# A sequence layer with an FFT convolution and a dense layer: the second norm's epsilon moves from VectorE to GpSimd, and all instructions stand in another order

## The chip, the core and the metric

The kernel runs on one core of one Trainium2 chip. The metric is the time of one execution in microseconds (us) of device time; less is better. The core's engines are named as the profile names them: PE is TensorE (matmuls; PEld its weight loads), DVE is VectorE, ACT is ScalarE, POOL is GpSimd, SP is SyncE, which here issues nearly all DMAs.

## What is computed

There are 2048 rows of 640 channels, all bf16. The reference, cut to its core:

```python
def _layernorm(x, eps=1e-5):
    return (x - mean(x)) / sqrt(var(x) + eps)

def _A_ref(q, k, v, shift_k, ssm_k, ssm_D):
    k_shift = sum(k_pad[:, t:t + S, :] * shift_k[:, ks - 1 - t] for t in range(4))
    kv = k_shift * v
    y = causal_convolution(kv, ssm_k)          # written as rfft, product, irfft over 2 * S
    return q * (y + kv * ssm_D)

def _B_ref(x, w1, b1, w2):
    h = x @ w1 + b1                            # 640 -> 1728
    return (h * tanh(softplus(h))) @ w2        # mish, 1728 -> 640

x = A_q
h = x + _A_ref(_layernorm(x), A_k, A_v, A_shift_k, A_ssm_k, A_ssm_D)
return h + _B_ref(_layernorm(h), B_w1, B_b1, B_w2)
```

So there is a first norm (of x), a long convolution, a gate and a sum, a second norm (of h), and a dense layer with Mish.

## The kernel before

The convolution is a Fourier transform in matmuls. The channels are cut into five chunks of 128. The stages, with the names that the order uses for their operations (`pe` at the end is the TensorE part, `ev` the copy of its PSUM result to SBUF, the eviction):

- **k1**: the filter `ssm_k` is transposed, one operation a chunk (L374).
- **s1k**: the first transform of the filter, 20 operations of 16 matmuls (L394, L395), each with an eviction of 128x1024.
- **kt**: the rows of `k` are transposed, 5 chunks of 8 fp32 transposes (L339), each chunk with one eviction of 2048 bf16 columns (`ktev`). **ks** makes the shifted sum, 10 operations of 16 matmuls (L355, L356); **kv** multiplies it with `v` on VectorE (L360), 10 operations. `wsh` and `ktsh` on GpSimd prepare both.
- **s2k**: a multiplication of all chunks of the filter with a table G, 22 operations of 6 matmuls (L420; the last has 2), evictions of 128x960 (the last 128x320). It needs all 20 s1k evictions.
- **s1v**, **s2v** (named s2v0, s2v1, s2v2 after the chunks they hold): the same two steps for the products k v, 20 operations each, evictions of 128x1024.
- **sw**: ten DMAs swap halves of the filter's spectrum; they need all s2k evictions. **pr**: 20 spectral products on VectorE (L459).
- **i1** (L477, 20 operations with evictions of 128x1024) and **i2** (L529, one for each of 16 tiles of 128 rows, eviction `y` of 128x640): the way back. i2 needs all i1.
- Per tile t: **ln1_t** takes the first norm's statistics on VectorE (L508, L509), **ln1p** turns them into a scale and a bias on GpSimd (L513 adds epsilon, L514 raises to the power -0.5, L515), **lnx** applies them (ScalarE L520 or GpSimd L522). **wb** and **h** (L536, L538) gate and add. **bn** takes the second norm's statistics (L542, L543) and adds epsilon (L544, VectorE), **pow** raises to -0.5 (L546, GpSimd), **hc** normalizes (L548, VectorE). Tiles 0 and 1 are transposed on TensorE (`trpe`, evicted by `trev`), the others by DMA (`tr`, L561).
- Dense layer: units of 256, 256, 512, 512, 512 rows. **m1** (L586, L593) is the first matmul, seven operations a unit, **hb** (L608) Mish on ScalarE, **m2** (L651, L659) the second matmul, **res** (L673, L676) the last sum on VectorE, **d_out** the store.

The order is one list, `ORDER`. Each word is an operation; all instructions are issued in the order of the list, each on its engine, and every engine works through its own in that order. `@n` gives the PSUM buffer of a TensorE operation: there are four, each 1024 fp32 columns wide, and a buffer is free for the next `@n` when the eviction of the one before has ended. `:d`, `:a`, `:p` put an operation on VectorE, ScalarE or GpSimd; without a letter an eviction of s1, s2, i1 or i2 runs on ScalarE. So the list decides which engine evicts what, which buffer is waited for, and in which order the DMAs are issued (SP too works through its own in order).

```python
EV = ["act", "dve"]
o.eng = _LETTER[eng] if eng else o.engs[0]
if o.psum is not None:
    o.psum.slot = int(slot)
```

Of the kernel before, what the change touches and what calls it, by code (L numbers as in the profile page):

```python
# [34 lines left out]
s2kev_18 kv1_0 kspe4_0@3 s2kev_12 s2kpe_90@1 kv4_0 s2kpe_54@0 s2kev_90 kspe3_1@2 s2kev_54 s2kpe_60@3 kv3_1 s1vpe0_3@1 s2kev_60 s2kpe_78@0 kspe2_1@2
s1vev0_3 s2kev_78:d s2kpe_102@3 s2kpe_0@1 kv2_1 s2kev_102 kspe2_0@0 s2kev_0 s2kpe_66@3 d_x3 kv2_0 s1vpe1_3@2 s2kev_66 s1vpe3_2@1 s1vev1_3:d d_x1
s1vpe3_0@0 s1vev3_2 s1vpe1_1@3 d_x0 d_x2 s1vev3_0 s1vev1_1:d s1vpe0_0@2 s2kpe_120@1 s1vev0_0 s1vpe2_2@0 s2kev_120:d s1vpe1_2@3 s1vev2_2 s1vpe2_0@2
s1vev1_2:d s1vpe1_0@1 s1vev2_0 s2kpe_6@0 d_t2m s2kpe_72@3 s1vev1_0 s2kev_6:d s2kpe_48@2 s2kev_72 s2kpe_96@1 s2kev_48:d s2v0pe_16@0 s2kev_96 s2kpe_84@3
s2v0ev_16:d s2kpe_30@2 s2kev_84 s1vpe4_2@1 ln1_3 s2kev_30 s2kpe_42@0 s2kpe_126@3 s2kev_42 s2kev_126:d s2kpe_108@2 ln1p3 ln1_0 s1vpe4_1@3 s2kev_108
s1vpe4_0@0 s1vev4_1:d s1vev4_2 ln1p0 s1vpe4_3@2 sw0_0 sw0_1 s1vev4_0 s1vev4_3:d s1vpe2_3@1 sw3_0 s1vpe3_3@3 lnx3:p s1vev2_3 sw1_1 s1vpe3_1@0  # L40
s1vev3_3:d s1vpe2_1@2 sw4_1 s1vev3_1 s2v0pe_0@1 lnx0:p sw2_1 ln1_1 s2v0pe_96@3 s1vev2_1 sw1_0 s2v0pe_80@0 sw3_1 ln1_2 s2v0ev_96 ln1p1 s2v0pe_64@2
sw2_0 s2v0ev_80 s2v0ev_0:d sw4_0 s2v0pe_32@3 lnx1:p s2v0ev_64 s2v0pe_112@0 pr0_0 ln1p2 s2v0pe_48@1 s2v0ev_112 s2v2pe_0@2 s2v0ev_32:d lnx2:p s2v0ev_48
s2v2pe_112@0 pr0_64 s2v2ev_112 s2v2pe_80@3 s2v1pe_64@1 s2v2ev_0 pr0_96 s2v2ev_80 s2v2pe_96@0 pr0_32 s2v2pe_32@2 s2v2ev_96 s2v2pe_64@3 pr1_96 s2v2ev_64
s2v2pe_16@0 pr1_64 s2v2ev_32 i1pe0_0@3 s2v1ev_64 s2v2pe_48@2 pr1_32 s2v2ev_48 i1pe0_3@1 pr1_0 s2v2ev_16 s2v1pe_0@2 pr3_32 i1ev0_0 s2v1pe_96@0 i1ev0_3
pr3_96 s2v1pe_32@3 s2v1ev_0 pr3_64 i1pe0_2@1 d_w12 s2v1ev_32 d_w11 i1pe0_1@2 pr4_96 d_w10 i1ev0_2 d_w13 i1pe1_2@3 pr3_0 d_w14 i1ev0_1 i1pe1_3@1
i1ev1_2 pr2_64 i1pe1_0@2 s2v1ev_96 pr2_0 i1pe3_0@3 i1ev1_3 i1pe3_2@0 pr2_32 i1ev1_0 i1pe3_1@1 pr4_64 i1ev3_0 i1pe3_3@2 i1ev3_1 pr2_96 i1pe1_1@3
# [4 lines left out]
hc2 pow3 y9 m1pe0_1@0 ln1_12 tr2 y5 w2z hb0_0 m1pe0_4@1 hc3 wb9 ln1p5 tr3 hb0_1 wb4 m1pe0_2@2 hb0_4 ln1_11 ln1p8 lnx5 m1pe0_5@3 wb7 hb0_2 ln1p12
ln1_10 m1pe0_6@0 hb0_5 m1pe1_6@1 h4 ln1p11 lnx12 ln1_15 m1pe1_0@2 hb1_6 ln1p10 ln1_14 lnx11 m1pe1_3@3 bn4 hb0_6 ln1p15 hb1_0 m1pe1_5@1 hb1_3 wb5
m1pe1_2@0 h7 hb1_5 wb6 h6 m1pe1_4@2 lnx15:p hb1_2 bn7 pow4 m1pe1_1@3 hb1_4 h5 pow7 hc4 i2pe11@1 bn6 hb1_1 ln1p14 tr4 i2pe12@0 m2pe0@2 y12 h9 lnx14:p
hc7 lnx10 bn9 pow6 y11 lnx8 hc6 pow9 bn5 tr6 m2pe2@3 wb14 pow5 tr7 hc9 wb10 wb11 tr9 wb8 hc5 h10 tr5 h8 wb15 bn8 m2pe1@0 h11 pow8 bn10 hc8 pow10 res0
m1pe2_6@1 h15 d_out0 ln1_13 tr8 m1pe2_1@2 hc10 ln1p13 hb2_6 res2 tr10 bn11 lnx13:p m1pe2_3@3 h14 hb2_1 pow11 wb12 hc11 h12 tr11 bn15 m2pe3@1 hb2_3
d_out2 wb13 pow15 bn14 hc15 pow14 bn12 tr15 m1pe3_6@2 h13 pow12 bn13 m1pe2_0@3 hc14 pow13 hb3_6 res3 res1 d_out3 hc12 d_out1 m1pe2_4@1 hc13 tr14 hb2_0
tr13 m1pe3_4@2 hb2_4 tr12 m1pe2_2@0 hb3_4 m1pe3_1@3 hb2_2 m1pe3_5@1 hb3_1 m1pe2_5@2 m1pe3_3@0 hb2_5 m1pe3_0@3 hb3_3 hb3_5 m1pe3_2@2 hb3_0 m2pe5@0
hb3_2 m2pe7@1 m2pe4@3 res7 res5 d_out7 d_out5 m2pe6@2 m1pe4_0@1 res6 res4 d_out4 d_out6 m1pe4_2@0 hb4_0 m1pe4_6@2 m1pe4_1@3 hb4_6 hb4_2 m1pe4_3@1
# [110 lines left out]
def kernel(  # L169
# [333 lines left out]
    for t in range(NT):  # L503
# [36 lines left out]
        def bnf(e, t=t):  # L540
            for hh in range(2):
                nc.vector.bn_stats(st2[:, t, hh, :], xt(t)[:, hh * 320:(hh + 1) * 320])  # L542
            nc.vector.bn_aggr(mv2[:, t, :], st2[:, t, :, :])  # L543
            nc.vector.tensor_scalar(ve2[:, t:t + 1], mv2[:, t, 1:2], EPS, None, ALU.add)  # L544
# [1 line left out]
        o_pw = OP(f"pow{t}", "pool", [o_bn, o_small], emit=lambda e, t=t: nc.gpsimd.tensor_tensor(r2[:, t:t + 1], ve2[:, t:t + 1], mhalf[:], ALU.pow))  # L546
        o_hc = OP(f"hc{t}", "dve", [o_pw] + ([trs[t - 7]] if t >= 7 else list(ks_pes.values())),
                  emit=lambda e, t=t: nc.vector.tensor_scalar(hc_s[t % 7], xt(t), mv2[:, t, 0:1], r2[:, t:t + 1], ALU.subtract, ALU.mult))  # L548
# [173 lines left out]
```

## Time and profile before

| what | us |
|---|---|
| median of 3 runs (lowest, highest) | 226.48 (226.25, 226.64) |
| the profiled execution's own time | 226.59 |
| its span, first to last instruction | 224.7 |
| first matmul of m1 starts | 99.94 |
| first matmul of m2 starts | 116.73 |
| last res starts | 221.78 |

A table by stage gives, for a stretch of time, the busy time of each engine, the number of its instructions behind an x, the granted TensorE clock, the busy share of the DMA engines and what they moved. A timeline row gives start, duration, engine, line, operation, output and inputs with shapes, and how many such instructions are merged in it; in brackets stands how long the engine idled ahead of it and what ended the wait. A group row has, behind the bar, the busy time of the group, the mean in ns of one, and idle time ahead of it. A matmul's printed duration holds its way through the array, so matmuls overlap: the distance from start to start is what one costs. The granted clock is 1.00 in all stretches.

### The profile page before, as it was taken

How to read it: one execution, taken by the hardware profiler on the slowest of the kernel's cores; microseconds unless marked ns; L12 is line 12 of the kernel's file. 1: busy time of each engine (PE TensorE's matmuls, PEld its weight loads, DVE VectorE, ACT ScalarE, POOL GpSimd, SP SyncE). 2: the span in 40 equal slices, each digit the busy share in tenths (PEclk: the TensorE clock that was granted, in tenths of full speed). 3: DMA queues.
4: the chain of work that ended last, by engine and by line, in shares of the span. 5: the costliest groups of instructions: out<-in, count | busy, mean ns of one | idle time of the engine just before them, and what ended most of it. 6: DMA issues, size and time to landing. Idle time of an engine off the chain costs nothing.

```text
span 224.7 us, 6128 instructions
## 1 busy us (share of the span) xinstructions
PE 214.4 (95%) x2644; PEld 157.3 (70%) x2650; DVE 137.6 (61%) x250; ACT 131.6 (59%) x178; POOL 58.5 (26%) x106
## 2 busy tenths in 40 slices
...
GB/s 177 386 414 416 417 369 16 139 340 276 417 417 18 274 125 158 254 0 58 5 29 76 59 98 67 128 18 0 3 0 58 40 21 0 0 20 29 88 29 73
DMA packets 19563, 30.98 MB, mean 138 GB/s; under 512 B 10704, under 2 KB 14928, under 8 KB 18768
## 3 DMA queue, kind: packets, MB, share of 16 engines
...
q10 hardware_dynamic: 336, 0.12, 0.3%
...
## 4 chain that ended last, share of the span: by engine, by line
PE 65%; DVE 11%; ACT 10%; DMA 6%; POOL 3%; issue 2%; SPq 0%; DVEq 0%; POOLq 0%
PE ps L651 26%; PE ps L586 22%; ACT uv L259 8%; DVE ks L459 6%; DMA rb<-in_A_q_dram 4%; PE ps L394 3%; DMA ks<-in_A_ssm_k_dram 2%; PE ps L339 2%; PE ps L355 2%; PE ps L420 2%; PE ps L374 2%; PE ps L356 2%; PE ps L395 1%; PE ps L593 1%; PE ps L659 1%
## 5 line engine op out<-in xcount | busy, mean ns | idle before, releaser
L608 ACT ACTIVATE ks<-ps,b1s 128x512 bf16<-128x512 f32 (+1 forms) x69 | 36.2, 599 | 47.9 <-PE ps L586 30.7
L651 PE MATMUL ps<-ks 128*128 128x320 bf16 (+2 forms) x420 | 58.6, 299 | 0.0
L586 PE MATMUL ps<-G 128*128 128x512 bf16 (+1 forms) x319 | 57.5, 336 | 0.8 <-ACT ks L608 0.5
L651 PEld LDWEIGHTS <-ks 128*128 128x128 bf16 x420 | 40.6, 98 | 17.4 <-issue 1.3
L586 PEld LDWEIGHTS <-G 128*128 128x128 bf16 x325 | 31.2, 98 | 25.3 <-issue 1.3
L259 ACT CAST uv<-ps 128x1024 bf16<-128x1024 f32 x49 | 45.7, 1099 | 0.1
L676 DVE TENSOR_TENSOR rb<-ps,rb 128x640 bf16<-128x640 f32 x15 | 11.8, 820 | 50.5 <-PE ps L659 48.1
L259 ACT CAST ks<-ps 128x960 bf16<-128x960 f32 (+2 forms) x46 | 37.7, 912 | 7.9 <-PE ps L395 5.9
L459 DVE TENSOR_TENSOR ks<-ks,uv 128x2048 bf16<-128x2048 bf16 x20 | 23.4, 1239 | 0.0
L420 PEld LDWEIGHTS <-G 128*128 128x128 bf16 x512 | 20.6, 96 | 3.6 <-issue 2.9
L477 PE MATMUL ps<-a_t,ks 128*128 128x128 bf16 x320 | 19.0, 219 | 0.9 <-ACT uv L259 0.5
L477 PEld LDWEIGHTS <-ks 128*128 128x128 bf16 x320 | 18.4, 113 | 1.5 <-issue 0.5
L513 POOL TENSOR_SCALAR ve<-mv 128x1 f32<-128x1 f32 x16 | 4.6, 289 | 47.7 <-DVE mv L509 46.7
L546 POOL TENSOR_TENSOR r<-ve,mhalf 128x1 f32<-128x1 f32 x16 | 10.8, 675 | 16.9 <-DVE ve L544 16.8
L420 PE MATMUL ps<-uv,G 128*128 128x64 bf16 (+1 forms) x384 | 12.7, 186 | 1.7 <-ACT uv L259 1.3
L508 DVE BATCH_NORM_STATS2 st<-rb 128x6 f32<-128x320 bf16 x32 | 13.8, 472 | 0.8 <-DMA rb<-in_A_q_dram 0.8
L542 DVE BATCH_NORM_STATS2 st<-rb 128x6 f32<-128x320 bf16 x32 | 14.0, 480 | 0.1
L261 DVE CAST ks<-ps 128x1024 bf16<-128x1024 f32 (+2 forms) x12 | 13.2, 1127 | 1.4 <-PE ps L395 0.7
L261 DVE CAST uv<-ps 128x1024 bf16<-128x1024 f32 x11 | 13.1, 1205 | 0.1
L673 DVE TENSOR_TENSOR rb<-ps,rb 128x384 bf16<-128x384 f32 (+1 forms) x2 | 1.0, 492 | 19.9 <-PE ps L651 19.9
L360 DVE TENSOR_TENSOR ra<-ps,rb 128x1024 bf16<-128x1024 f32 x10 | 11.9, 1219 | 1.3 <-PE ps L356 0.7
L522 POOL TENSOR_SCALAR ra<-rb,r,nmr 128x640 bf16<-128x640 bf16 x10 | 12.1, 1212 | 1.2 <-PE ps L395 0.6
...
## 6 DMA issues: line engine op xcount, KB each, us to landing
...
G<-in_B_w_dram SPq DMA_DIRECT2D x5, 432.0 KB, 5.5
```

What stands on the lines that cost most here:

```text
L259: nc.scalar.copy(o, i)
L261: nc.vector.tensor_copy(o, i)
L360: nc.vector.tensor_tensor(kv_w[:, m, :, 8 * h:8 * h + 8, :], p_.f32().rearrange("p (l t d) -> p d t l", l=4, t=8), raw_v[:, 8 * h:8 * h + ...
L420: nc.tensor.matmul(p_.f32()[:, o:o + n], g_v[:, f, :], src[:, :, f, :], start=True, stop=True)
L459: nc.vector.tensor_tensor(o, o, v, ALU.mult)
L477: nc.tensor.matmul(pz[:, dgl, :], KS[:, k, b, :, l], a12[:, k, :], start=k == 0, stop=k == 1)
L508: nc.vector.bn_stats(st1[:, t, hh, :], xt(t)[:, hh * 320:(hh + 1) * 320])
L522: nc.gpsimd.tensor_scalar(lnx_s[t % 9], xt(t), r1[:, t:t + 1], nmr1[:, t:t + 1], ALU.mult, ALU.add)
L542: nc.vector.bn_stats(st2[:, t, hh, :], xt(t)[:, hh * 320:(hh + 1) * 320])
L586: nc.tensor.matmul(ph[:, o:o + w], w1[:, dc, fc * P:fc * P + P], lt[:, dc, 0:w], start=dc == 0, stop=dc == NDC - 1)
L608: nc.scalar.activation(hb[:, fc, 0:n], p_.f32()[:, i * 512:i * 512 + n], ACT.Mish, bias=b1s[:, fc:fc + 1], scale=1.0)
L651: nc.tensor.matmul(p_.f32()[:, o:o + n], lhs, w2[:, k, cols:cols + n], start=fc == 0, stop=single and fc == 13)
```

## The change

The addition of epsilon in `bn` goes from VectorE (L544) to GpSimd, in front of the power, where the first norm has it already. `hc` gets a second form on ScalarE, which the constant `HC_ACT = ()` leaves unused.

```diff
-            nc.vector.tensor_scalar(ve2[:, t:t + 1], mv2[:, t, 1:2], EPS, None, ALU.add)
         o_bn = OP(f"bn{t}", "dve", [o_h], emit=bnf)
-        o_pw = OP(f"pow{t}", "pool", [o_bn, o_small], emit=lambda e, t=t: nc.gpsimd.tensor_tensor(r2[:, t:t + 1], ve2[:, t:t + 1], mhalf[:], ALU.pow))
...
+        def pwf(e, t=t):
+            nc.gpsimd.tensor_scalar(ve2[:, t:t + 1], mv2[:, t, 1:2], EPS, None, ALU.add)
+            nc.gpsimd.tensor_tensor(r2[:, t:t + 1], ve2[:, t:t + 1], mhalf[:], ALU.pow)
+            if t in HC_ACT:
...
+        o_pw = OP(f"pow{t}", "pool", [o_bn, o_small], emit=pwf)
```

The whole list `ORDER` is another one: the same 660 operations in other places, with other buffers and, in part, other engines. Its first part, up to the first operations of s1v, reads before and after:

```diff
-d_dr wz idn d_n0 cz wm@0 small lane d_n1 d_cst d_sk d_n2 warm d_n4 d_n3 kz d_g7 dsel dcol dadd0 d_k0 k1pe0@1 dadd1:p d_k3 k1pe1@2 d_k1 k1ev0b d_k2
-k1ev0 s1kpe0_2@3 k1ev1 s1kpe0_1@0 s1kev0_2 dadd2:p d_v2 s1kpe0_0@1 s1kev0_1 s1kpe1_2@2 dadd4:p d_a12 s1kpe0_3@3 s1kev1_2:d k1pe2@0 s1kev0_3 d_v1 dadd3
...
-s1kpe4_0@2 s1kev2_2 s1kpe2_0@3 s1kev4_0:d d_g2 s1kpe3_2@0 s1kev2_0 s1kpe3_3@1 wsh2 s1kev3_2:d s1kpe3_0@2 d_g1 ktpe4_0@3 s1kev3_0 ktpe4_3 s1kev3_3:d
-ktpe4_1 ktpe1_0@0 ktpe1_1 ktpe1_3 d_g3 ktpe1_2 ktpe4_2 ktev1:a ktpe0_0@2 ktev4 ktpe0_2 ktpe0_1 ktpe2_0@1 d_g0 ktpe0_3 ktpe2_2 ktev0 s1kpe4_3@3 d_g5
...
-kv0_0 s1kpe2_3@2 s1kpe4_2@1 kv0_1 s1kev2_3 ktsh3 kspe4_1@3 ktsh2 s1kev4_2 s1kpe3_1@2 kv4_1 s1vpe0_2@0 s1kev3_1 s1kpe2_1@1 s1vev0_2:d s1vpe0_1@3
-s1kev2_1 kspe1_1@2 s1vev0_1 s2kpe_36@0 kv1_1 s2kpe_114@1 s2kev_36 kspe3_0@3 s2kev_114:d s2kpe_24@2 kspe1_0@0 s2kev_24 kv3_0 s2kpe_18@1 s2kpe_12@2
+d_dr wz idn d_n0 cz wm@0 small lane d_n1 d_cst d_sk d_n2 warm d_n3 d_n4 d_g0 dsel dcol dadd0 d_k2 k1pe0@1 d_k3 dadd1:p k1pe1@2 d_a12 k1ev0b d_k0 k1ev0
+s1kpe0_3@3 k1ev1 s1kpe0_1@0 s1kev0_3 d_k1 s1kpe0_0@1 dadd2 s1kev0_1 s1kpe1_3@2 s1kev0_0:d dadd3:p d_g4 s1kpe0_2@3 k1pe2@0 s1kev0_2 dadd4:p d_g1
+s1kev1_3 kz b1pe@1 k1pe4@3 k1ev2 c_b1 cfpe@2 k1pe3@1 k1ev4:a coef d_v0 s1kpe2_0@0 k1ev3 wsh1 s1kpe2_1@2 s1kev2_0 s1kpe4_3@3 d_g7 s1kev2_1:d s1kpe3_1@1
...
+s1kpe4_0@3 s1kev3_3 s1kpe1_1@2 ktsh0 s1kev4_0:d d_v3 s1kpe4_2@1 wsh0 s1kev1_1 s1kpe3_0@0 s1kev4_2:d s1kpe2_3@3 s1kev3_0 d_g3 ktpe4_0@2 ktpe4_2 ktpe4_3
+s1kev2_3 ktsh1 ktpe3_0@1 ktpe4_1 ktpe3_3 ktev4 ktpe3_1 ktpe3_2 s2kpe_6@0 s2kpe_12@3 ktev3 s2kev_6 kspe0_0@2 s2kev_12 s2kpe_18@0 kv0_0 ktsh3 kspe2_0@1
+s2kev_18 ktsh4 s2kpe_42@3 kv2_0 kspe3_0@2 s2kev_42 s2kpe_96@0 kv3_0 s2kpe_24@1 s2kev_96 kspe4_0@3 s2kev_24 kspe1_0@2 kv4_0 s2kpe_108@0 kspe1_1@1 kv1_0
...
+s2kev_54 s2kpe_60@3 s2kev_84 ln1_0 kspe2_1@1 s2kev_60 s2kpe_48@0 kv2_1 ln1p0 s1vpe0_2@2 s2kev_48 s1vpe1_1@3 s1vev0_2:d s1vpe2_1@1 d_x2 s1vev1_1
```

The handover to the dense layer reads, from the first `y` to the first m1:

```diff
-i2a2@0 y0 i2b1 i2pe8@3 y1 wb0 i2pe4@2 h0 y8 i2pe14@1 wb1 y4 bn0 i2pe15@3 y14 i2b2 i2a3@2 y2 i2b3 h1 i2pe13@1 pow0 y3 bn1 i2pe6@0 lnx9:p y15 i2pe7@2
-y13 wb2 i2pe10@3 pow1 y7 hc0 i2pe9@1 h2 y6 trpe0@2 hc1 wb3 trev0:a trpe1@0 bn2 trev1:a i2pe5@2 y10 m1pe0_3@0 h3 pow2 lnx4 bn3 lnx7:p m1pe0_0@3 hb0_3
+i2b0 i2pe4@2 y0 wb1 i2pe5@1 y4 h1 i2pe8@3 wb0 y5 h0 i2b2 i2a3@2 y8 bn1 i2pe15@1 y2 i2b3 i2pe12@3 bn0 y15 pow1 i2pe13@0 y3 i2pe11@1 pow0 y12 hc1 wb2
+trpe1@2 y11 i2pe7@3 hc0 y13 h2 trpe0@1 trev1:a wb3 i2pe6@0 bn2 trev0:a i2pe10@2 y7 m1pe0_3@1 h3 lnx11 pow2 bn3 m1pe0_2@3 y6 hc2 y10 pow3 ln1_7
```

What the new list does by count, taken from the whole of it:

| operations | before | after |
|---|---|---|
| s2k evictions on ScalarE / VectorE | 16 / 6 | 19 / 3 |
| s1v evictions on ScalarE / VectorE | 13 / 7 | 11 / 9 |
| s2v evictions on ScalarE / VectorE | 17 / 3 | 19 / 1 |
| ktev on ScalarE / VectorE | 2 / 3 | 1 / 4 |
| s1k and i1 evictions on ScalarE / VectorE | 33 / 7 | 33 / 7 |
| lnx on ScalarE / GpSimd | 6 / 10 | 8 / 8 |
| s2k operations ahead of the last kv / behind it | 12 / 10 | 20 / 2 |
| s1v operations ahead of the last kv | 3 | 0 |
| ln1 ahead of the first pr, y, m1, m2 | 4, 10, 10, 15 | 4, 10, 10, 15 |

The bias `b1` is transposed and copied (`b1pe`, `c_b1`) before the first k1 of chunk 4 instead of ahead of the first y. Most loads of G stand among those of v instead of behind them. The loads of the first two quarters of x stand ahead of the last four kv instead of behind all ten, and the load of the table `t2m`, which i2 needs, stands behind the swaps and the loads of `w1` in SP's queue instead of ahead of the swaps.

More of the change, by code (lines that the diff above doesn't have):

```diff
@@ L35 @@
[L35 to L46, printed above, removed]
@@ L51 @@
[L51 to L58, printed above, removed]
@@ new lines @@
+s2v0ev_112:d s2v0pe_80@1 sw3_1 s2v0ev_32 s1vpe3_1@0 lnx1:p sw0_1 ln1_2 s1vpe4_0@2 s2v0ev_80 sw3_0 s1vpe3_3@3 sw4_1 ln1_3 s1vev3_1 ln1p2 s1vpe2_3@1
+sw2_0 s1vev4_0 s1vev3_3:d sw2_1 s1vpe4_2@0 lnx2:p s1vev4_2 s2v0pe_96@2 pr1_64 ln1p3 s2v0pe_16@3 s2v0ev_96 s2v2pe_32@0 s1vev2_3:d lnx3:p s2v0ev_16
+s2v2pe_80@2 pr1_96 s2v2ev_32 s2v2pe_112@1 s2v2pe_64@3 s2v2ev_112 pr1_0 s2v2pe_48@0 s2v2ev_64 s2v2pe_0@1 pr0_96 s2v2ev_0 s2v2pe_16@3 pr1_32 s2v2ev_16
+s2v1pe_96@1 pr0_64 s2v2ev_48 i1pe1_1@3 s2v2ev_80 s2v2pe_96@0 pr3_0 s2v1ev_96 i1pe1_2@2 pr3_32 i1ev1_1 s2v1pe_64@1 pr0_32 s2v2ev_96 s2v1pe_0@3 i1ev1_2
@@ new lines @@
+i2b0 i2pe4@2 y0 wb1 i2pe5@1 y4 h1 i2pe8@3 wb0 y5 h0 i2b2 i2a3@2 y8 bn1 i2pe15@1 y2 i2b3 i2pe12@3 bn0 y15 pow1 i2pe13@0 y3 i2pe11@1 pow0 y12 hc1 wb2
+trpe1@2 y11 i2pe7@3 hc0 y13 h2 trpe0@1 trev1:a wb3 i2pe6@0 bn2 trev0:a i2pe10@2 y7 m1pe0_3@1 h3 lnx11 pow2 bn3 m1pe0_2@3 y6 hc2 y10 pow3 ln1_7
+m1pe0_1@0 tr2 lnx8 ln1p10 hc3 hb0_3 m1pe0_5@2 wb8 tr3 hb0_2 h8 ln1p7 m1pe0_6@1 ln1_9 hb0_5 m1pe0_4@3 hb0_1 ln1p14 ln1_15 m1pe0_0@2 hb0_6 lnx4 wb6 w2z
+m1pe1_0@0 wb11 lnx10 wb4 lnx7:p hb0_4 m1pe1_4@1 ln1_5 ln1p15 hb1_0 m1pe1_5@3 wb7 hb0_0 h4 ln1p5 hb1_4 m1pe1_3@0 bn8 hb1_5 lnx5:p m1pe1_1@2 ln1_13
@@ L73 @@
 D_FIRST = True
+HC_ACT = ()
 PAIRS = False
@@ L217 @@
     r2 = cpool.tile([P, NT], F32, name="r2")
+    nmr2 = cpool.tile([P, NT], F32, name="nmr2")
     a12_t = cpool.tile([P, 256], BF16, name="a12_t")
```

36 lines of the change are left out of this document (26 added, 10 removed).

## The prediction, as it was put on record

> **What bounds the kernel now.** I read the page's totals first, then the table by stage, cut where the work changes hands: 44 us (first transforms of k v run alone), 91.9 (first y), 99.9 (first m1), 116.7 (first m2).
>
> ```profile
> span 224.7 us, 6128 instructions
> PE 214.4 (95%) x2644; PEld 157.3 (70%) x2650; DVE 137.6 (61%) x250; ACT 131.6 (59%) x178; POOL 58.5 (26%) x106
> ```
>
> ```profile
> 8.00:44.00 36.00, 35.72 (x761) 34.01 (x761) 31.65 (x32) 30.70 (x31) 11.53 (x11) 1.00 0.77 303
> 44.00:91.90 47.90, 43.98 (x976) 40.35 (x973) 46.62 (x62) 47.58 (x53) 16.08 (x28) 1.00 0.70 262
> 91.90:99.90 8.00, 7.67 (x60) 4.51 (x59) 7.36 (x22) 7.97 (x14) 2.81 (x5) 1.00 0.22 79
> 99.90:116.70 16.80, 16.28 (x150) 13.59 (x148) 14.97 (x45) 15.38 (x34) 14.08 (x28) 1.00 0.20 21
> 116.70:225.00 108.30, 104.72 (x670) 61.52 (x674) 34.36 (x83) 28.51 (x46) 10.33 (x16) 1.00 0.16 43
> ```
>
> Columns are length, busy PE, PEld, DVE, ACT, POOL, clock, DMA share, GB/s. Read the fifth number, ACT: from 44 to 99.9 it is busy 47.58 of 47.90 and 7.97 of 8.00 us, so there the end of a stage is the sum of ScalarE's work. From 116.7 on PE is the bound, with the same matmuls in both kernels. So the time can change in three places: when ScalarE arrives at its dense stretch and with how much left; the handover to m1; and the first dense units up to 116.7.
>
> In the first 44 us ScalarE idles 36 - 30.70 = 5.3 us (0.7 of them before its first eviction). Its timeline tells why:
>
> ```profile
> 20.67 1.87 ACT L259 COPY uv<-ps 128x2048 bf16<-128x2048 bf16 x1 [0.86 <-PE ps L339]
> 22.93 1.01 ACT L259 CAST ks<-ps 128x1024 bf16<-128x1024 f32 x1 [0.40 <-PE ps L395]
> 25.01 1.86 ACT L259 COPY uv<-ps 128x2048 bf16<-128x2048 bf16 x1 [1.07 <-PE ps L339]
> 33.38 0.96 ACT L259 CAST ks<-ps 128x960 bf16<-128x960 f32 x1 [0.61 <-PE ps L420]
> 42.93 3.76 ACT L259 CAST uv<-ps 128x1024 bf16<-128x1024 f32 x4
> 48.39 5.32 ACT L259 CAST ks<-ps 128x960 bf16<-128x960 f32 x6
> 53.50 38.07 ACT L259 CAST uv<-ps 128x1024 bf16<-128x1024 f32 x41
> 91.92 6.66 ACT L259 CAST ks<-ps 128x640 bf16<-128x640 f32 x11 [0.28 <-PE ps L529]
> 98.51 1.38 ACT L259 COPY G<-ps 128x640 bf16<-128x640 bf16 x2
> ```
>
> It waits for PE (brackets), for the transposes of k above all. The last rows are dense and give what one eviction costs: (91.37 - 53.50) / 41 = 0.92 us for 128x1024, where 91.37 is 53.50 + 38.07 less some 0.2 by which the last one outlasts its step; (53.50 - 48.39) / 6 = 0.85 for 128x960; (98.51 - 91.92) / 11 = 0.60 for a y.
>
> **The change, part by part.**
>
> *Epsilon.*
>
> ```profile
> L544 DVE TENSOR_SCALAR ve<-mv 128x1 f32<-128x1 f32 x16 | 2.5, 154 | 0.6
> L513 POOL TENSOR_SCALAR ve<-mv 128x1 f32<-128x1 f32 x16 | 4.6, 289 | 47.7 <-DVE mv L509 46.7
> L546 POOL TENSOR_TENSOR r<-ve,mhalf 128x1 f32<-128x1 f32 x16 | 10.8, 675 | 16.9 <-DVE ve L544 16.8
> L514 POOL TENSOR_TENSOR r<-ve,mhalf 128x1 f32<-128x1 f32 x16 | 9.4, 586 | 1.3
> ```
>
> VectorE loses 16 x 154 ns = 2.5 us, GpSimd gets 16 x 289 ns = 4.6 us. GpSimd is 26% busy; what is queued there behind a pow are ln1p and lnx for later tiles. A chain is not longer: the first norm has the new form already.
>
> ```profile
> 52.62 0.22 DVE mv L509
> 53.22 0.58 POOL r L514
> 94.97 0.22 DVE mv L543
> 95.45 0.72 POOL r L546
> ```
>
> From the start of the aggregate to the end of the power it takes 53.80 - 52.62 = 1.18 us with the addition on GpSimd, and 96.17 - 94.97 = 1.20 with it on VectorE. So a tile's chain changes by nothing; what is gained is room on VectorE, 0.154 us a tile.
>
> A port could make it dearer. These are ln1p2's addition and lnx2, which run beside pr on VectorE:
>
> ```profile
> 61.00 1.06 POOL L513 TENSOR_SCALAR ve<-mv 128x1 f32<-128x1 f32 x1
> 63.18 3.93 POOL L522 TENSOR_SCALAR ra<-rb,r,nmr 128x640 bf16<-128x640 bf16 x1
> L536 DVE TENSOR_TENSOR ks<-ks,ra 128x640 bf16<-128x640 bf16 x16 | 7.5, 482 | 0.4 <-ACT ks L259 0.4
> ```
>
> The addition took 1.06 us in place of 0.289. The Trainium skill, SBUF — State Buffer, section "Who interferes with whom", says that a VectorE instruction with two SBUF inputs and a GpSimd instruction that reads SBUF exclude each other: the one that comes second waits for all of the first. The two rows agree with that. By that rule an addition that meets a wb or an h can wait for all of it; this is the third rival, priced by the row of L536.
>
> *First 44 us, TensorE.* I walked the new order by hand, operation by operation: each starts when the one ahead of it on its engine, its inputs and its buffer allow, with the steps of the rows. Up to 13.9 us both orders do the same transposes of the filter and five s1k or so. The steps:
>
> ```profile
> 18.76 3.55 PE ps L339 x28
> 31.31 0.84 PE ps L420 x12
> 28.39 0.24 PE L394 MATMUL ps<-cst,ks 128*64 128x128 bf16 x1
> 30.35 0.23 PE L355 MATMUL ps<-rw,uv 128*128 128x128 bf16 x1
> 31.98 0.22 PE L355 MATMUL ps<-rw,uv 128*128 128x128 bf16 x1
> 32.77 0.30 PE L420 MATMUL ps<-ks,G 128*128 128x160 bf16 x2
> ```
>
> A transpose of k costs 3.55 / 28 = 0.127 us, an s2k operation 0.84 / 2 = 0.42, an s1 operation (30.35 - 28.39) / 4 = 0.49 (four stand between), a ks operation 32.77 - 31.98 = 0.79. After 13.9 us the new order does 15 s1k (7.4 us) and 40 transposes (5.1): 26.4. Then come only s2k and ks, in turns: 10 x 0.79 + 19 x 0.42 + 0.14 = 16.1, so 42.5; with waits for buffers, 0.6 by my walk, the first s1v starts at 43.1. ScalarE stands behind it with two s2k evictions and takes its first s1v at 44.3. In this stretch TensorE is the bound, ScalarE idles 3.3 us in my walk (before 4.6), because only one ktev is left to it and the transposes stand between s1k. Loads are the same bytes in another order.
>
> ```profile
> GB/s 177 386 414 416 417 369 16 139 340 276 417 417 18 274 125 158 254 0 58 5 29 76 59 98 67 128 18 0 3 0 58 40 21 0 0 20 29 88 29 73
> ```
>
> A slice is 224.7 / 40 = 5.6 us: 0.99 + 2.17 + 2.33 = 5.5 MB by 16.9 us. The filter, one part of G, k and the small tables ahead of them are 5.9 MB, in by about 18 us; the transposes start at 18.5 and use the last quarter of k at 20. That is close, but in time; v and the rest of G (5.7 MB more, 14 us at 415 GB/s) are in piece by piece up to 33, each ahead of its use.
>
> *44 to 91.9, ScalarE.* Before, from 42.93 up to the last i1 eviction, it had 11 s1v + 17 s2v + 18 i1 and 6 s2k to do: 46 x 0.92 + 6 x 0.85 = 47.4, so the last starts at 90.3, and the first y 1.6 later (91.92). After, from 44.3: 11 + 19 + 18 = 48 x 0.92 + one s2k 0.85 = 45.0, so 89.3, and y at 89.3 + 1.4 = 90.7 (the copy of b1 is gone from between). **Minus 1.2 us.** VectorE must keep up.
>
> ```profile
> L459 DVE TENSOR_TENSOR ks<-ks,uv 128x2048 bf16<-128x2048 bf16 x20 | 23.4, 1239 | 0.0
> L261 DVE CAST uv<-ps 128x1024 bf16<-128x1024 f32 x11 | 13.1, 1205 | 0.1
> ```
>
> They overlap by some 0.1, so 1.14 us each. From the last kv at 44.1: 9 s1v, 1 s2v and 20 pr (30 x 1.14), an s2k and 3 ln1 (about 1.05 each): 38.4, so pr ends at 82.5 (before 85.2), 7 us ahead of the last i1 eviction. The statistics that move are no gain of their own: four ln1 stand ahead of the first pr and ten ahead of the first y in both orders, and VectorE has room there. Moved DMAs: the swaps are issued about 1.2 us earlier; t2m comes behind the w1 loads.
>
> ```profile
> ra<-tab_t2m SPq DMA_DIRECT2D x1, 1024.0 KB, 8.5
> G<-in_B_w_dram SPq DMA_DIRECT2D x5, 432.0 KB, 5.5
> ```
>
> The last s2v matmul, for which w1 waits, comes at about 72.4; five issues later t2m goes, at 75, and lands by 8.5 us at 83.5, or, if w1's 5.5 come first, at 86 to 89. It is needed at 89. Cost zero, with little room at the far end.
>
> *Handover.* 11 y x 0.60 and two trev 1.38 stand on ScalarE ahead of m1 in both orders: 8.0 us. The pair of chains bn1, bn0 to hc0 comes in time for trev0, with 0.1 to spare. I take **minus 0.1** (the wait of 0.16 between the last y and trev0 goes).
>
> *First dense units.*
>
> ```profile
> 107.75 0.45 PEld L586 LDWEIGHTS <-G 128*128 128x128 bf16 x5 [0.78 <-DMA G<-rw]
> ```
>
> PE waits here for the rows of tile 3. hc3 stands behind two bn that are 0.154 shorter each, counted from the first m1: 0.3, and a little for the order. **Minus 0.4**; bounds 0 and 0.78. ScalarE has two more lnx, one of them ahead of the first m2; its sum there, 3 y, 5 lnx and 27 hb halves, still ends with the matmuls. After that hc and tr stay 2 us or more ahead of their m1.
>
> Sum: -1.2 - 0.1 - 0.4 = -1.7 us. The profiled execution took 226.59 (span 224.7 and 1.9 around it), 0.11 above the median of 226.48. So **224.8** against the median.
>
> **The rivals.** Measurement tells 0.2%, 0.45 us, from no change: below 226.03 is faster, above 226.93 slower.
>
> *Four buffers are too few for the turns (slower).* Between 26.4 and 43 us each buffer goes from TensorE to VectorE or ScalarE and back, ks and s2k in strict turns; before, s1v operations stood between. Break even: there are ten ks turns; if each loses 0.17 us more than my walk gives, the 1.7 are gone. The wait of 0.61 at 33.38 is the price of one such turn gone wrong; half of it, 0.3 at each of ten turns, is +3.0: 226.5 - 1.7 + 3.0 = 227.8. For it: 33.38 itself; against it: PE was busy without a gap there before, and the rows' steps leave ScalarE idle, not TensorE.
>
> *The idle stays.* ScalarE idles 4.6 us as before and has 0.3 us more work (two s2k and a small one more, one ktev less): front +0.3 instead of -1.2, with the rest 226.3: no change.
>
> *The port.* pow0's addition meets wb2, as the order has it, and loses one L536, 0.48. With 0.1 to spare m1 starts 0.4 later: 225.2.
>
> *It does nothing by itself.* Epsilon alone is worth -0.3, and the statistics' move nothing; if the order's front didn't matter we would see 226.2. This is within the second case.
>
> **How the numbers follow.** Forecast 0.58, too few buffers 0.22, idle stays 0.12, port 0.08. Faster: forecast 0.57, port 0.08, part of idle stays 0.03: 0.68. Same: 0.08 of idle stays and 0.03 of the edges: 0.11. Slower: 0.21. The forecast's own range is 223.4 (the wait of 0.78 and another 1 us of ScalarE's idle go) to 226.0. The range for 8 in 10 reaches up into the slower case to half its chance: 223.4 to 227.6.
>
> **What would show it.** Right: ScalarE's busy time in the first 44 us is about 32 of 36; the first s2k eviction starts at about 27 us (31.8 before), the first s1v on ScalarE at 44.3, the first y at 90.7, the first m1 at 98.6, m2 at 115.0; GpSimd's new addition means under 0.35 us and the power under 0.6; no wait of PE for i2's table. Wrong: gaps on PE between 27 and 43; ScalarE idle behind 44; hc0 later than trev1; a time above 226.

## The result, and the profile after

| | before | after |
|---|---|---|
| median of 5 runs each (lowest, highest), us | 226.64 (226.25, 227.25) | **225.25** (225.11, 225.33) |
| the profiled execution's own time, us | 226.59 | 225.33 |

The ratio is 0.994, with a 95% interval of 0.9925 to 0.9955: faster by 0.6%, 1.4 us against the before measured beside it and 1.2 us against the median of 226.48 that the prediction started from. The forecast was 224.8 in a range of 223.4 to 227.6. In kernels with the changed code the lines up to bn stand two higher than before (evictions L261 and L263, i2 L531), those behind it eleven or twelve (hc L559, tr L573, m1 L598).

The page's totals after:

```profile
span 223.5 us, 6119 instructions
PE 214.0 (96%) x2645; PEld 157.6 (70%) x2650; DVE 133.2 (60%) x232; ACT 133.0 (59%) x182; POOL 58.9 (26%) x120
```

The table by stage of after, cut at the same hand-overs as that of before (first y 91.51, first m1 99.49, first m2 115.54):

```profile
8.00:44.00 36.00, 35.67 (x693) 34.10 (x691) 30.58 (x34) 31.14 (x34) 11.92 (x17) 1.00 0.84 327
44.00:91.50 47.50, 43.91 (x1046) 40.86 (x1044) 46.13 (x59) 47.15 (x52) 15.08 (x28) 1.00 0.70 258
91.50:99.50 8.00, 7.42 (x61) 4.30 (x60) 6.87 (x19) 7.99 (x14) 2.33 (x6) 1.00 0.01 2
99.50:115.50 16.00, 16.00 (x151) 13.67 (x149) 13.64 (x39) 15.67 (x35) 13.02 (x28) 1.00 0.11 22
115.50:223.50 108.00, 104.78 (x671) 61.44 (x674) 33.49 (x77) 29.53 (x47) 13.12 (x30) 1.00 0.17 44
```

Compare lengths with the rows of before. The second stage is 0.4 shorter, the third as long as it was, and the fourth, from m1 to m2, is 0.8 shorter, with PE busy in all 16.00 us of it (16.28 of 16.80 before). The last stage is the same work in both. From milestone to milestone, each in the profiled execution:

| stretch | before | after | difference | predicted |
|---|---|---|---|---|
| start to the first s1k eviction on ScalarE | 8.71 | 9.01 | +0.30 | 0 |
| from there to the first y | 83.21 | 82.50 | -0.71 | -1.2 |
| first y to first m1 | 8.02 | 7.98 | -0.04 | -0.1 |
| first m1 to first m2 | 16.79 | 16.05 | -0.74 | -0.4 |
| first m2 to the last res | 105.05 | 105.04 | -0.01 | 0 |

So the sum was nearly right for reasons that were not: the front gave 0.7 of the 1.2 that was forecast (0.4 with the later start), and the first dense units gave nearly twice their 0.4. That the two errors cancel is luck. The experiments ask where both parts come from.

### The profile page after: what moved, and what is told of

It reads as the page before. It is cut to its first block, busy times and chain, and to the rows that moved or that the text cites. A ratio compares the mean times of both kernels' runs of the same rounds, so it can differ in the third digit from the quotient of the medians.

```text
span 223.5 us, 6119 instructions
## 1 busy us (share of the span) xinstructions
PE 214.0 (96%) x2645; PEld 157.6 (70%) x2650; DVE 133.2 (60%) x232; ACT 133.0 (59%) x182; POOL 58.9 (26%) x120
## 4 chain that ended last, share of the span: by engine, by line
PE 70%; DVE 13%; DMA 9%; ACT 4%; issue 2%; SPq 1%; POOL 1%; DVEq 0%
PE ps L663 26%; PE ps L598 25%; DVE ks L461 6%; DMA ks<-in_B_w_dram 4%; DMA ks<-ks 3%; PE ps L396 3%; PE ps L422 3%; ACT uv L261 3%; DMA ks<-in_A_ssm_k_dram 3%; PE ps L341 2%; PE ps L376 2%; DVE ks L263 2%; PE ps L357 2%; DVE ra L362 1%; PE ps L397 1%
## 5 line engine op out<-in xcount | busy, mean ns | idle before, releaser
L598 PE MATMUL ps<-G 128*128 128x512 bf16 (+1 forms) x320 | 57.0, 336 | 0.3
L598 PEld LDWEIGHTS <-G 128*128 128x128 bf16 x325 | 31.3, 98 | 24.4 <-issue 1.1
L261 ACT CAST uv<-ps 128x1024 bf16<-128x1024 f32 x49 | 45.2, 1197 | 0.0
L261 ACT CAST ks<-ps 128x960 bf16<-128x960 f32 (+3 forms) x49 | 39.8, 905 | 8.1 <-PE ps L397 5.0
L544 DVE BATCH_NORM_STATS2 st<-rb 128x6 f32<-128x320 bf16 x32 | 14.0, 478 | 0.1
L263 DVE CAST uv<-ps 128x1024 bf16<-128x1024 f32 x11 | 12.9, 1204 | 0.1
L524 POOL TENSOR_SCALAR ra<-rb,r,nmr 128x640 bf16<-128x640 bf16 x8 | 8.9, 1118 | 10.0 <-PE ps L397 9.3
L422 PE MATMUL ps<-ks,G 128*128 128x160 bf16 x128 | 11.2, 230 | 0.0
L396 PE MATMUL ps<-cst,ra 128*64 128x128 bf16 x160 | 10.6, 219 | 0.7 <-ACT uv L261 0.5
L263 DVE CAST ks<-ps 128x1024 bf16<-128x1024 f32 (+1 forms) x9 | 10.5, 1197 | 0.5 <-PE ps L422 0.3
```

The lines of the kernel that those rows point to most:

```text
L261: nc.scalar.copy(o, i)
L263: nc.vector.tensor_copy(o, i)
L396: nc.tensor.matmul(ps[0:64, dgl, :], lhs, mc, start=True, stop=True)
L422: nc.tensor.matmul(p_.f32()[:, o:o + n], g_v[:, f, :], src[:, :, f, :], start=True, stop=True)
L598: nc.tensor.matmul(ph[:, o:o + w], w1[:, dc, fc * P:fc * P + P], lt[:, dc, 0:w], start=dc == 0, stop=dc == NDC - 1)
```

## The experiments

The engine theory is the prediction's: the order shortens the front, and epsilon, taken from VectorE, makes hc3 and so the rows of tile 3 earlier by 0.3; epsilon alone is then worth 0.3. The fetch theory came from the trace of DMA packets: in before, the wait of PE for tile 3's rows (0.78) falls together with a fetch of instructions over the same DMA engines, and what after gains there it gains because its transposes no longer meet this fetch. The letters in the first two expectations mean something else: A there says that the order makes the gain, B that VectorE's relief makes it. Times below are medians, the ratio is that to the kernel before on the same chip.

### Epsilon alone, order alone

Epsilon alone is the changed code with the list `ORDER` of before; order alone is before's code with the new list.

```diff
-            nc.vector.tensor_scalar(ve2[:, t:t + 1], mv2[:, t, 1:2], EPS, None, ALU.add)
+            nc.gpsimd.tensor_scalar(ve2[:, t:t + 1], mv2[:, t, 1:2], EPS, None, ALU.add)
```

```diff
-d_dr wz idn d_n0 cz wm@0 small lane d_n1 d_cst d_sk d_n2 warm d_n4 d_n3 kz d_g7 dsel ...
+d_dr wz idn d_n0 cz wm@0 small lane d_n1 d_cst d_sk d_n2 warm d_n3 d_n4 d_g0 dsel ...
...
```

> Epsilon on GpSimd, the order of before. Theory A (the order makes the gain, epsilon alone nearly none): 226.2 to 226.6, first m1 at 99.8 to 100.0, the first dense units 16.0 to 16.8 long. Rival B (VectorE's relief makes it): 225.2 to 225.6, with the first y before 91.6.

> The new order, epsilon still on VectorE (16 additions of 154 ns). Theory A: 225.2 to 225.5, first y at 91.5 as in after, hc0 no longer waits 0.46 for pow0. Rival B: 226.2 to 226.6, the first dense units as long as before (16.8).

Measured: epsilon alone 226.69, ratio 1.0005 (0.9994 to 1.0017); order alone 226.37, ratio 0.9993 (0.9979 to 1.0007); before had 226.58. Neither alone can be told from no change, though both together give 0.994; so A fails in the second run and B in the first. For epsilon alone the prediction's 0.3 us is too much: the interval reaches 0.14 us to the fast side. Here are the groups of hc and of GpSimd's two instructions in epsilon alone:

```profile
L559 DVE TENSOR_SCALAR rw<-rb,mv,r 128x640 bf16<-128x640 bf16 x16 | 7.3, 461 | 3.5 <-POOL r L550 3.4
L550 POOL TENSOR_TENSOR r<-ve,mhalf 128x1 f32<-128x1 f32 x16 | 9.3, 584 | 1.3
L549 POOL TENSOR_SCALAR ve<-mv 128x1 f32<-128x1 f32 x16 | 4.9, 308 | 13.3 <-DVE mv L545 13.1
```

and hc in before:

```profile
L548 DVE TENSOR_SCALAR rw<-rb,mv,r 128x640 bf16<-128x640 bf16 x16 | 6.9, 438 | 1.4 <-POOL r L546 1.3
```

The last figures are what VectorE waited for the power: 3.4 us in place of 1.3. Of the 2.5 us that its 16 additions cost, VectorE gives back 2.1 as waits, since the chain itself is no shorter.

In order alone the front did come 0.7 earlier (first eviction to first y 82.54), but PE then waits:

```profile
99.20 7.26 PE L586 MATMUL ps<-G 128*128 128x256 bf16 x65
107.64 7.26 PE L586 MATMUL ps<-G 128*128 128x256 bf16 x65 [1.18 <-DMA G<-rw]
116.59 1.39 PE L651 MATMUL ps<-ks 128*128 128x320 bf16 x9
```

The first unit needs 256 rows, tiles 0 and 1; then 1.18 us pass until tile 3's rows have landed, and m2 starts 17.39 after m1 (before 16.79). In after there is no such bracket:

```profile
99.49 14.35 PE L598 MATMUL ps<-G 128*128 128x256 bf16 x130
113.77 0.74 PE L605 MATMUL ps<-G 128*64 128x256 bf16 x10
115.54 2.47 PE L663 MATMUL ps<-ks 128*128 128x320 bf16 x17
```

So order alone gains 0.7 in the front and loses 0.6 behind m1. What lies on the DMA engines while the two transposes run is a view of the DMA queues over their stretch. In before (102.4 to 107.7 us):

```profile
q1 hardware_dynamic: 1344, 0.33, 60.0%
q8 instruction: 1, 0.02, 1.7%
q14 instruction: 1, 0.01, 0.8%
...
G<-rw SPq DMA_TRANSPOSE x2, 4.3
```

and in after (101.7 to 105.4):

```profile
q1 hardware_dynamic: 1344, 0.33, 44.4%
...
G<-rw SPq DMA_TRANSPOSE x2, 2.6
```

The same 1344 packets, but before has two packets of the kind "instruction" among them and 4.3 us from issue to landing, after none and 2.6. That is the coincidence that the fetch theory starts from; it took experiments that move the fetch by itself to make it a cause.

### One half of the new order each

The list was cut ahead of the first i2: front_new has the new list up to there and then what is left in before's order and on before's engines, tail_new the reverse; both have epsilon on GpSimd.

```diff
-i1ev2_1 i1ev4_3:d i1pe4_2@0 i1ev4_0 lnx6:p i1pe4_1@2 ln1_4 i1ev4_2 ln1p11 i2a1@1 d_w2a i1ev4_1 ln1_14 i2a0@3 d_w2b ln1p4 d_w2c i2b1 ln1_10 i2a2@0 y1
...
+i1ev2_1 i1ev4_3:d i1pe4_2@0 i1ev4_0 lnx6:p i1pe4_1@2 ln1_4 i1ev4_2 ln1p11 ln1_9 ln1p9 ln1_7 i1ev4_1:d ln1p4 i2a0@2 d_w2b ln1_5 i2a1@1 d_w2a ln1p7
...
```

(front_new against after; the lines that follow are before's.)

> The new order up to the first i2, then the order of before; epsilon on GpSimd. If the front makes the gain (the prediction's first term, 1.2): 225.4 or less, first y 0.4 to 1.2 earlier than before's 91.9. If most of the gain is in the first dense units (0.74 of 1.2 by the two traces): 226.0 to 226.3, with a wait for tile 3's rows near 107 as in before unless the transposes meet no code fetch.

> The order of before up to the first i2, then the new one; epsilon on GpSimd. If most of the gain is in the first dense units: 225.6 to 225.9, no wait for tile 3's rows. If the front makes it: 226.2 to 226.6. All four traces also tell whether the first filter load lands later with the new order (5.36 against 5.12 us so far): with the new front in order_only and front_new if it is the order, in any if it is chance.

Measured: 229.63, ratio 1.0136 (1.0118 to 1.0155), and 228.68, ratio 1.0099 (1.0075 to 1.0123). Both times miss every expectation and answer nothing, because the cut changed more than it should. The two lists take the statistics of different tiles ahead of the first y, so a cut list has eleven (front_new) or twelve (tail_new) ln1 there instead of ten. They also put different i1 evictions on VectorE, so a cut list has two there instead of one, and the last one stands behind three ln1 (front_new) or two (tail_new). VectorE's timeline of front_new, then what PE does:

```profile
88.48 0.88 DVE L510 BATCH_NORM_STATS2 st<-rb 128x6 f32<-128x320 bf16 x2
...
91.50 1.18 DVE L263 CAST uv<-ps 128x1024 bf16<-128x1024 f32 x1
```

```profile
92.73 3.52 PE L531 MATMUL ps<-uv,ra 128*128 128x512 bf16 x23 [3.30 <-DVE uv L263]
```

The eviction, on ScalarE in after (`i1ev4_1`), waits behind three ln1 on VectorE (88.48 to 91.50, 1.0 each), and i2 waits 3.3 us for it. For the wait behind m1 the traces come out as expected: front_new has it, with the fetch among its transposes, and tail_new does not (table further down).

### The fetch moved by the warm-up

Instructions added at the start shift which matmul a fetch falls on. The warm-up was rewritten with more and smaller matmuls: 30 more in before (60 PE instructions with their weight loads), and 15 more in after, where 19 stands for the 34.

```diff
-WARM = 9
+WARM = 5
...
+        for _ in range(34):
+            nc.tensor.matmul(wm_p.f32()[:, 0:16], wz[:, 0:P], wz[:, P:P + 16], start=True, stop=True)
```

> The kernel before with 30 more matmuls in the warm-up (5 of 512 columns and 34 of 16 in place of 9 of 512), so that all of PE's later code is fetched 60 instructions earlier. Theory: the 16 KB fetch at 104.65, which held up the transposes of tiles 2 and 3 (landing 4.8 and 3.8 us after issue, against 2.4 elsewhere), comes some 3 us earlier and misses them: they land in 2.4 to 2.8 us, PE's wait of 0.78 ahead of unit 1 goes, the time falls by 0.4 to 0.8 to about 225.8. Rival (hc3 is late by the order of VectorE): the wait stays at 0.6 to 0.8, time within 0.3 of before.

> The changed kernel with 15 more matmuls in the warm-up (5 of 512 columns and 19 of 16), so that the fetch at 105.42 comes some 1.6 us earlier, among the transposes' packets (103.0 to 105.3). Theory: they land 1 to 2 us later, PE waits 0.3 to 0.8 for tile 3's rows ahead of unit 1, the time rises by as much, to 225.6 to 226.0. Rival: no wait, 225.25 within 0.2.

Measured: before_shift 227.96, ratio 1.0064 (1.0041 to 1.0087); after_shift 226.61, ratio 0.9991 (0.9973 to 1.001). In before_shift the fetch came at 102.8, ahead of the transposes, these landed in 2.48 and 3.08 us, the wait went, and m1 to m2 took 16.11 in place of 16.79, as the fetch theory had it. But the first eviction came at 9.83, 1.1 later: the longer warm-up cost more than the fetch. After_shift left no trace to compare. Both times lie outside what either theory expected, and as timings both are inconclusive; a better place for the extra instructions was needed.

### The port and the handover

In after, hc0 waits for pow0, whose addition and power run beside hc1 and wb2. GpSimd and VectorE in after:

```profile
95.38 0.22 POOL L549 TENSOR_SCALAR ve<-mv 128x1 f32<-128x1 f32 x1 [3.35 <-DVE mv L545]
95.69 0.57 POOL L550 TENSOR_TENSOR r<-ve,mhalf 128x1 f32<-128x1 f32 x1
96.38 0.40 POOL L549 TENSOR_SCALAR ve<-mv 128x1 f32<-128x1 f32 x1
96.86 0.70 POOL L550 TENSOR_TENSOR r<-ve,mhalf 128x1 f32<-128x1 f32 x1
```

```profile
96.29 0.45 DVE L559 TENSOR_SCALAR rw<-rb,mv,r 128x640 bf16<-128x640 bf16 x1
96.67 0.48 DVE L538 TENSOR_TENSOR ks<-ks,ra 128x640 bf16<-128x640 bf16 x1
97.61 0.45 DVE L559 TENSOR_SCALAR rw<-rb,mv,r 128x640 bf16<-128x640 bf16 x1 [0.46 <-POOL r L550]
```

The first pair, alone, takes 0.22 and 0.57; the second 0.40 beside hc1 and 0.70 beside wb2, and hc0 waits 0.46. The experiment put wb2 behind hc0 and filled PE with the i2 of tile 6 meanwhile:

```diff
-... i2pe11@1 pow0 y12 hc1 wb2
-trpe1@2 y11 i2pe7@3 hc0 y13 h2 trpe0@1 trev1:a wb3 i2pe6@0 bn2 ...
+... i2pe11@1 pow0 y12 hc1
+trpe1@2 y11 i2pe7@3 i2pe6@0 hc0 wb2 y13 h2 trpe0@1 trev1:a wb3 bn2 ...
```

By mistake the i2 of tile 6 stands in tile 13's buffer ahead of y13, so y13 reads tile 6's result.

> The changed kernel with i2 of tile 6 ahead of trpe0 instead of behind it, and wb2 behind hc0 instead of ahead of it. The prediction's third rival (the port) says: pow0's addition and power took 0.40 and 0.70 us because wb2 ran beside them; alone they take 0.22 and 0.57 as pow1's did, and hc0 starts 0.3 earlier. Then the first m1 starts at 99.25 (bounded by trev0's end) instead of 99.49; time 225.0. If the port is not the reason, pow0 stays at 1.1 to 1.2 us and only the moved i2 gains, 0.1 to 0.2.

Measured: 226.16, ratio 0.9979 (0.9969 to 0.999), slower than after's 0.994 (its interval touches that of after_again below). Two new waits make it so, on ScalarE and on PE:

```profile
98.21 0.69 ACT L261 CAST ks<-ps 128x640 bf16<-128x640 f32 x1 [0.81 <-PE ps L531]
```

```profile
99.55 0.70 PE L531 MATMUL ps<-uv,ra 128*128 128x512 bf16 x4 [1.10 <-ACT G L261]
```

y13 waits for the i2 of tile 6, and the next i2 for a buffer that trev1, behind y13 on ScalarE, frees; m1 comes 8.81 after the first y (7.98). For the port the run still tells something: without wb2 beside it pow0's power took 0.57 instead of 0.70, its addition beside hc1 still 0.40. So the meeting with wb2 cost 0.13, and hc0 stood 0.14 earlier behind the first y (5.96 in place of 6.10), not the 0.3 that was expected. The Trainium skill, SBUF — State Buffer, section "Who interferes with whom", counts an operation of hc's kind (tensor_scalar) among those that can take the shared ports as well, if its operands meet certain conditions. The 0.18 that the addition lost beside hc1, with wb2 away, agrees; whether hc meets the conditions no run here shows.

### After once more, and the fetch moved in the middle of the kernel

Three kernels issue some matmuls of s2v0 twice, with the same result: the copies run on PE in a stretch where ScalarE is the bound, and shift every later fetch. order_fetch is order alone with 64 instructions more (four matmuls in each of eight s2v0, each with its weight load), before_fetch is before with the same 64, after_fetch is after with 16, chosen to put the fetch back among the transposes (1 in place of the 4 below). after_again is after unchanged.

```diff
                 for f in ...:
-                    nc.tensor.matmul(p_.f32()[:, o:o + n], g_v[:, f, :], src[:, :, f, :], start=True, stop=True)
+                    for _ in range(2 if name == "s2v0" and f - f0 < 4 else 1):
+                        nc.tensor.matmul(p_.f32()[:, o:o + n], g_v[:, f, :], src[:, :, f, :], start=True, stop=True)
```

> The changed kernel once more, beside the three that follow, on their chip. Ratio to before as measured first: 0.994, or 225.2 to 225.5 where before is 226.6. If the fetch decides by tenths of a us (its packet came 0.15 us behind the transposes' last one in the first trace), single executions may catch it: then the runs spread over 0.7 us and the ratio lies between 0.994 and 0.998.

> The new order with epsilon on VectorE (order_only), and four matmuls of each of the eight s2v0 operations issued twice (32 matmuls, 64 PE instructions, the result unchanged), so that the fetch comes at about 101.6 instead of 105.1, ahead of the transposes. Theory (the fetch took the gain of the order): tile 3 lands 2.4 to 2.8 us after its issue instead of 4.2, the wait of 1.18 goes, m2 starts at 115.4 to 115.7 instead of 116.6, time 225.2 to 225.6. Rival (epsilon's place makes the difference between order_only and after): wait and time as in order_only, 226.2 to 226.5.

> The changed kernel with one matmul of each s2v0 operation issued twice (8 matmuls, 16 PE instructions), so that the fetch comes at about 104.5 instead of 105.4, while tile 3's packets are under way. Theory: tile 3 lands 3.7 to 4.3 us after issue, PE waits 0.3 to 0.8 ahead of unit 1, the time rises by as much over the changed kernel beside it. Rival: no wait, the same time within 0.2.

> The kernel before with four matmuls of each s2v0 operation issued twice (64 PE instructions), so that the fetch comes at about 101.2 instead of 104.65, without the longer start that the changed warm-up had. Theory: tiles 2 and 3 land 2.4 to 3.0 us after issue, the wait of 0.78 goes, m1 to m2 16.1 instead of 16.8, time 0.5 to 0.8 below before. Rival: no change.

Measured, before 226.35 on this chip: after_again 225.57, ratio 0.9956 (0.9938 to 0.9974); order_fetch 225.64, 0.9955 (0.9939 to 0.9972); after_fetch 225.54, 0.9955 (0.9939 to 0.9972); before_fetch 226.14, 0.9993 (0.9969 to 1.0017).

**order_fetch decides.** It has epsilon on VectorE as order alone has; only the fetch is elsewhere, and its ratio is that of the whole change. The wait of 1.18 is gone:

```profile
99.36 14.35 PE L587 MATMUL ps<-G 128*128 128x256 bf16 x130
113.64 0.74 PE L594 MATMUL ps<-G 128*64 128x256 bf16 x10
115.40 2.61 PE L652 MATMUL ps<-ks 128*128 128x320 bf16 x18
```

Its DMA queues over the transposes (101.8 to 106 us) hold no instruction packet:

```profile
q1 hardware_dynamic: 1344, 0.33, 34.6%
...
G<-rw SPq DMA_TRANSPOSE x2, 2.4
```

And after_fetch brings the collision back (101.5 to 107 us), with a wait that after doesn't have:

```profile
q1 hardware_dynamic: 1344, 0.33, 69.0%
q8 instruction: 1, 0.02, 1.1%
...
G<-rw SPq DMA_TRANSPOSE x2, 4.1
```

```profile
106.98 7.26 PE L599 MATMUL ps<-G 128*128 128x256 bf16 x65 [0.22 <-DMA G<-rw]
```

All kernels with a trace to compare, from the records of DMA packets and landings, the fetch counted from the first m1:

| kernel | fetch of 16 KB starts | tile 2, tile 3: issue to landing | m1 to m2 |
|---|---|---|---|
| before | +4.7, among the transposes | 4.77, 3.81 | 16.79 |
| epsilon alone | +4.6, among them | 2.67, 3.89 | 16.86 |
| order alone | +5.9, among them | 2.47, 4.20 | 17.39 |
| after_fetch | +4.3, among them | 4.56, 3.67 | 16.44 |
| front_new | +4.5, among them | 4.70, 3.58 | 16.58 |
| after | +5.9, just behind them | 2.67, 2.59 | 16.05 |
| after_again | +6.4, behind them | 2.66, 2.59 | 16.06 |
| order_fetch | +1.5, ahead of them | 2.47, 2.40 | 16.04 |
| before_fetch | +2.2, ahead of them | 2.47, 3.09 | 16.10 |
| before_shift | +1.7, ahead of them | 2.48, 3.08 | 16.11 |
| handover | +5.8, behind them | 2.67, 2.59 | 16.05 |
| tail_new | +6.1, behind them | 3.27, 2.69 | 16.05 |

In the seven without the fetch among the transposes m1 to m2 takes 16.04 to 16.11, in the five with it 16.44 to 17.39, whatever the order and wherever epsilon is added. In all five the first weight load of unit 1 starts 0.1 us behind the landing of tile 3's rows (in before 107.75 and 107.64), also where the profile names another engine or none as the releaser, and the fetch had ended by then (in order alone at 106.32). So PE waited for the rows and not for its own instructions. (A landing of 3.1 to 3.3 in a row without the fetch has a fetch of 8 KB from another queue, q14, beside it, in before_fetch at 104.75; the instructions added to PE did not move that one, 104.74 in before.)

order_fetch shows one thing more: epsilon on VectorE can have a price behind m2. From there to the last res it takes 105.52 us, in the eleven other traces 105.04 or 105.05, and PE waits for a res. The first two rows are of order_fetch, the last one is the same pair of res in after:

```profile
139.30 7.71 PE L587 MATMUL ps<-G 128*128 128x512 bf16 x35 [0.32 <-DVE rb L677]
138.44 1.54 DVE L677 TENSOR_TENSOR rb<-ps,rb 128x640 bf16<-128x640 f32 x2
136.69 1.50 DVE L688 TENSOR_TENSOR rb<-ps,rb 128x640 bf16<-128x640 f32 x2
```

VectorE, with its additions, is 1.75 us later there than in after; in order alone m2 came 1.2 later, and there is no such wait. This is read from the rows, no run tests it, and the times do not show it (order_fetch 225.64, after_again 225.57).

In times, only order alone and order_fetch show the collision, on two chips: 0.9993 (from 0.9979) and 0.9955 (up to 0.9972). For before and before_fetch the profile gives 0.7 us and the times 0.2 with an interval that reaches from 0.7 faster to 0.4 slower; for after and after_fetch the profile gives 0.4 slower and the times nothing. Both miss what the theory expected of the time. So in single executions the fetch's place is shown, and how often an unprofiled execution pays for it is not.

before_fetch and order_fetch differ in the list alone: epsilon on VectorE, the same 64 instructions added, no fetch of PE among the transposes of either profiled execution, one chip. All seven times of order_fetch (225.33 to 225.77) lie below all twelve of before_fetch (225.84 and up), by 0.5 us in the medians. So the new order, with the collision out of the way, gains about 0.5 us by itself.

## Why the prediction was right in size and wrong in two of its steps

**The first 44 us: mechanism right, a term mis-sized.** From the first s2k eviction to ScalarE's first s1v the walk had 17.3 us (about 27 to 44.3); it took 17.16. ScalarE's timeline of after:

```profile
9.01 3.76 ACT L261 CAST ks<-ps 128x1024 bf16<-128x1024 f32 x4 [5.00 <-PE ps L397]
...
23.19 3.77 ACT L261 CAST ks<-ps 128x1024 bf16<-128x1024 f32 x4
28.12 3.79 ACT L261 CAST ks<-ps 128x960 bf16<-128x960 f32 x4 [1.16 <-PE ps L422]
32.15 1.82 ACT L261 CAST ks<-ps 128x960 bf16<-128x960 f32 x2 [0.24 <-PE ps L422]
34.56 0.96 ACT L261 CAST ks<-ps 128x960 bf16<-128x960 f32 x1 [0.59 <-PE ps L422]
35.76 0.96 ACT L261 CAST ks<-ps 128x960 bf16<-128x960 f32 x1 [0.25 <-PE ps L422]
36.97 8.38 ACT L261 CAST ks<-ps 128x960 bf16<-128x960 f32 x10 [0.25 <-PE ps L422]
45.28 3.76 ACT L261 CAST uv<-ps 128x1024 bf16<-128x1024 f32 x4
```

Read the starts. The first s2k eviction stands at 28.12 where the walk had about 27, and all of the delay is already there: 0.30 from the start (9.01 in place of 8.71) and 0.7 from the step "after 13.9 us the new order does 15 s1k and 40 transposes: 26.4". PE in that stretch:

```profile
14.20:27.45 13.25, 13.20 (x288) 12.39 (x287) 10.24 (x11) 12.22 (x12) 9.91 (x7) 1.00 1.02 412
```

```profile
13.78 0.91 PE L376 MATMUL ps<-ident,ks 128*128 128x128 bf16 x12
```

PE is busy 13.20 of 13.25 us, and the profile names no wait of PE there: the steps are dearer. The filter's last transposes run up to 14.69, where the walk, 0.30 later, would be done at 14.2; from 14.69 to the first s2k matmul at 27.45 it is 12.76 for the 12.5 of the walk. Behind it, from 45.28 to the start of the last i1 eviction at 89.70 ScalarE took 44.4 for the predicted 45.0, and from there to y 1.8 for 1.4. Together +0.3 +0.7 -0.6 +0.4 against the walk: y at 91.5 and not 90.7. Of the loads, v and the rest of G (four parts and seven) are 6.3 MB and not 5.7, which cost nothing: no engine waits for them. The 0.30 at the start is hardly the order's: the first load of the filter landed between 5.09 and 5.40 in seven runs with the new front and between 5.04 and 5.33 in five with the old one, and after's own was one of the late ones (5.36, before 5.12).

ScalarE's busy time in the first 44 us rose to 31.14, a third of the way from 30.70 to the 32 that was named; the idle that stayed is the row of 1.16 at 28.12 above all. That much of the rival "the idle stays" was true.

**Too few buffers: fell.** PE is busy 15.90 of 16.00 us from 27 to 43, and the turns took what the walk gave.

**Epsilon: right.** The addition means 325 ns and the power 597 (named: under 0.35 and 0.6), and no load is waited for where i2 begins: the table t2m landed at 84.36.

**Handover: right within its 0.1**, and the port's mechanism was seen, though not its price. hc0 waited 0.46, but m1 stood behind two more i2 and the second trev, and came 7.98 behind y.

**First dense units: the step that failed.** The prediction had the wait of 0.78 for tile 3 as a matter of hc3's time, shortened by 0.3 through two shorter bn. hc3's time matters, but what made the rows late was the instruction fetch among the transposes, which no step names. With it among them neither the order nor epsilon gets rid of the wait (m1 to m2 takes 17.39 with the order alone, 16.86 with epsilon alone and still 16.44 with both, in after_fetch); in after the second transpose is issued 3.67 after the first m1 (before 3.89, order alone 4.10), which is early enough to end just ahead of the fetch. Epsilon's share in the 0.74 us, then, is that after's second transpose goes 0.4 us before order alone's, counted from the first m1; it decides only because the fetch follows 0.12 us behind the last packet.

**What stays open.** How often an unprofiled execution of before pays for the collision: the times of before_fetch and after_fetch show nothing of it, with intervals that would just hide the profiles' 0.7 and 0.4. And the seven tenths in the front are seen in each profile with the whole new list (82.50 to 82.63 from the first eviction to the first y), while no pair of runs measured the front by itself: both cut lists failed at that, and the 0.5 us of order_fetch against before_fetch are the whole list, with what it loses behind m2.
